# Second layers of four chunks as seven block products instead of eight, with x scaled before the transpose

## The chip, the cores and the metric

The kernel runs on one core of one Trainium2 chip. The metric is device time in microseconds for one execution of the whole kernel; lower is better. The engines are named as the profile names them: TensorE (PE) multiplies, VectorE (DVE), ScalarE (ACT) and GpSimd (POOL) do elementwise work, and SP issues transfers; GpSimd issues transfers on a queue of its own.

## The reference

```python
def _attn_ref(q, k, v, f_logit):                 # q, k, v, f_logit: (4, 8, 768, 48)
    f = 1.0 / (1.0 + np.exp(-f_logit))
    for t in range(S):
        state = f[:, :, t, :, None] * state + np.einsum('bhd,bhe->bhde', k[:, :, t], v[:, :, t])
        y[:, :, t] = np.einsum('bhd,bhde->bhe', q[:, :, t], state)

def _moe_ref(x, domain_probs, w1, w2):           # x: (3072, 384), w1: (4, 384, 1024), w2: (4, 1024, 384)
    p = domain_probs / (domain_probs.sum(-1, keepdims=True) + 1e-09)
    for e in range(E):
        h = np.maximum(x @ w1[e], 0.0)
        out += p[:, e:e + 1] * (h @ w2[e])

x = attn_out.transpose(0, 2, 1, 3).reshape(B * S, H * D)      # 3072 tokens of 384
```

A gated linear recurrence over 768 steps gives one row of 384 numbers for each token. Each row then goes through four experts of two layers, and the four results are added, weighted by probabilities.

## The kernel before, in words

The 768 steps are cut into six chunks of 128, numbered 0 to 5. A chunk holds 128 steps of each of the four batches, so 512 tokens. For every chunk there are two pieces of work.

*Attention* of a chunk, per batch `b`: the gates go through an exponential and a logarithm (`gate1`, `gate2` on ScalarE), are summed over the steps by a matmul (`pe_cs`, step `cs`), and exponentials of the sums (`exps`) scale q and k (`product`, mostly on GpSimd). Scaled q and k are transposed, in chunks 1 (second half) to 5 by a DMA transpose on SP (`dma_tp`, tile `QK`). Then come the scores (`pe_at`, step `at`), masked copies of them (`ev_at`, tile `AT`, on VectorE), the outputs (`pe_y`, step `y`), a bf16 copy of y (`yb`) and its DMA transpose into `xT` (`dma_xt`, three blocks of 128). `pe_kv`, `ev_kv` and `state` carry the recurrent state `Sf` and its bf16 copy `Sb` to the next chunk. v is loaded in float32 and cast (`cast_v`), except in chunk 0, where GpSimd's queue casts it in the transfer.

*Experts* of a chunk: the first layer `mm_h` makes 128 hidden rows for 512 tokens with three matmuls of 512 columns; `relu` copies them to `h` in bf16, on ScalarE or VectorE. There are 8 such units for each of 4 experts. The second layer `mm_o` makes 128 tokens x 384 outputs with eight matmuls of 384 columns. `ev_o` multiplies by the probability and adds to `o`; after the last expert the tile is stored. Chunk 1 is worked in halves of 256 tokens.

The attention of chunk c+1 is laid among the experts of chunk c. The order isn't written out by hand. A planner (`Plan`) gets every step with a cost for each engine that may do it, a priority, the steps that it depends on, and the buffers that it takes and frees (`rooms` says how many there are of each kind). `Plan.run` plays this through and hands out the steps: an engine that is free takes the step of lowest priority number that is ready. The instructions are then issued in that order on each engine, and each engine works its queue in order, so a step that is late holds up what stands behind it. `unit[0]` counts the units of expert work and serves as the scale of priorities; `base` sets where the attention of the next chunk begins on it. PSUM banks are in two pools of four: `ps_m` for the experts and `ps_t` for the attention.

The lines of the profile that matter below: L374 is the matmul of `mm_h`, L389 that of `mm_o`, L385 and L383 are `relu` on ScalarE and VectorE, L396, L398 and L400 are `ev_o`, L329 is `ev_at`, L336 and L340 are `pe_y`, L346 is `pe_kv`, L353 is `ev_kv`, L360 and L361 are `state`, L301 is `product`, L226 and L228 are copies (`yb` and others), L314 and L318 are the two DMA transposes, L237 and L233 are loads, L246 loads weights, L404 is the store.

## Time and profile before

| | before |
|---|---|
| median of 3 runs | 298.79 us (298.46 to 300.08) |
| span of the profiled execution | 296.6 us |
| TensorE matmuls busy in it | 289.0 us (97%), 2172 instructions |
| weight loads | 170.0 us (57%) |
| ScalarE | 174.3 us (59%), 317 instructions |
| VectorE | 126.1 us (43%), 250 instructions |
| GpSimd | 106.1 us (36%), 180 instructions |
| matmuls of the second layer (L389) | 776, 152.6 us |
| matmuls of the first layer (L374) | 708, 152.8 us |

The span is that of one profiled execution; the timed runs are of the same program, and their median lies 2.2 us above that span. Engines work at the same time, so busy times don't add up to the span. In the groups of the page, the time after the bar is the sum of the instructions, with the mean of one in ns, and then the idle time of that engine just before them. Matmuls follow each other in a pipeline, so the mean of one is longer than the distance from one to the next.

### The profile page before, as it was taken

The page shows a single profiled execution, that of the slowest core. Times are in us where ns is not written, and L with a number is a line of the kernel's source. Part 1 is how long each engine was busy: PE and PEld are TensorE (multiplying, and loading weights), DVE is VectorE, ACT ScalarE, POOL GpSimd, SP SyncE. Part 2 cuts the span into 40 slices and gives each one's busy share as a digit, 9 for nine tenths or more (in the row PEclk, how much of TensorE's full clock was granted, in tenths as well). Part 3 has the DMA queues.
Part 4 walks back from the last instruction along what each step waited for, and adds up shares of the span by engine and source line. Part 5 has one row for each costly group of instructions (what it writes and reads, how often), then busy time and mean ns, then how long its engine had stood idle before and what let it go on. Part 6 is the DMA issues. An engine that isn't in the chain of part 4 may idle for free.

```text
span 296.6 us, 5591 instructions
## 1 busy us (share of the span) xinstructions
PE 289.0 (97%) x2172; PEld 170.0 (57%) x2172; DVE 126.1 (43%) x250; ACT 174.3 (59%) x317; POOL 106.1 (36%) x180
## 2 busy tenths in 40 slices
PE   6899999999999999999999999999999999999995
PEld 2476555567777775555555555555555555555553
DVE  6786012785763673045375235243523222101223
ACT  5656656666684667777477575554475544465440
POOL 5786401138767448144449372243220000000000
PEclk9999999999999999999999999999999999999999
DMA  7999999998979999998979932102432100200002
GB/s 157 200 169 206 207 192 210 189 210 167 201 152 166 191 171 185 209 187 164 198 133 218 179 60 35 27 0 67 122 61 30 27 2 27 80 2 0 0 2 106
DMA packets 136462, 36.43 MB, mean 123 GB/s; under 512 B 126812, under 2 KB 135644, under 8 KB 136436
## 3 DMA queue, kind: packets, MB, share of 16 engines
q1 hardware_dynamic: 125188, 29.35, 52.0%
q0 software_dynamic: 11248, 6.72, 16.4%
q8 instruction: 17, 0.28, 0.4%
q14 instruction: 9, 0.07, 0.1%
HBM read 31.51 MB, written 4.72 MB: 122 GB/s over the span
## 4 chain that ended last, share of the span: by engine, by line
PE 78%; DMA 14%; POOL 3%; SPq 2%; issue 1%; ACT 1%; DVE 0%; POOLq 0%
PE ps_m L389 37%; PE ps_m L374 35%; DMA w_sb<-in_moe_w_dram 10%; DMA k<-in_k_dram 4%; SPq L237 2%; POOL w_sb L246 2%; PE ps_t L325 2%; PE ps_t L340 1%; PE ps_t L336 1%; PE ps_t L273 1%; POOL vb L233 1%; PE ps_t L346 1%; ACT e L293 1%; DVE o L396 0%; ACT xT L226 0%
## 5 line engine op out<-in xcount | busy, mean ns | idle before, releaser
L385 ACT ACTIVATE h<-ps_m 128x512 bf16<-128x512 f32 (+2 forms) x188 | 102.4, 548 | 91.9 <-PE ps_m L374 88.9
L374 PE MATMUL ps_m<-xT,w_sb 128*128 128x512 bf16 (+3 forms) x708 | 152.8, 339 | 0.6 <-ACT xT L226 0.6
L389 PE MATMUL ps_m<-w_sb,h 128*128 128x384 bf16 (+1 forms) x776 | 152.6, 324 | 0.1
L389 PEld LDWEIGHTS <-h 128*128 128x128 bf16 x776 | 75.0, 98 | 59.0 <-DMA w_sb<-in_moe_w_dram 0.3
L396 DVE SCALAR_TENSOR_TENSOR o<-ps_m,pn,o 128x384 f32<-128x384 f32 (+1 forms) x73 | 44.5, 612 | 117.3 <-PE ps_m L389 111.1
L374 PEld LDWEIGHTS <-w_sb 128*128 128x128 bf16 x708 | 65.3, 98 | 43.5 <-issue 0.7
L301 POOL TENSOR_TENSOR qk<-q,e 128x384 bf16<-128x384 f32 x18 | 21.4, 1195 | 36.5 <-ACT e L293 34.3
L360 POOL TENSOR_TENSOR Sf<-Sf,egs 48x192 f32<-48x192 f32 x40 | 20.2, 504 | 36.5 <-DVE Sf L353 34.4
L329 DVE TENSOR_TENSOR AT<-ps_t,mask 128x512 bf16<-128x512 f32 x48 | 30.2, 683 | 5.1 <-PE ps_t L325 5.1
L383 DVE TENSOR_SCALAR h<-ps_m 128x256 bf16<-128x256 f32 (+2 forms) x40 | 19.3, 499 | 26.5 <-PE ps_m L374 13.1
L293 ACT ACTIVATE e<-ps_t 128x384 f32<-128x384 f32 x48 | 26.7, 668 | 5.0 <-PE ps_t L273 3.5
L301 POOL TENSOR_TENSOR qk<-k,e 128x384 bf16<-128x384 f32 x20 | 20.2, 1013 | 8.7 <-ACT e L293 5.5
L353 DVE TENSOR_TENSOR Sf<-Sf,ps_t 48x192 f32<-48x192 f32 x40 | 14.0, 350 | 10.3 <-PE ps_t L346 9.4
L246 POOL DMA_DIRECT2D w_sb<-in_moe_w_dram x11 | 8.8, 807 | 18.5 <-DMA k<-in_k_dram 17.2
L361 POOL CAST sb<-Sf 48x192 bf16<-48x192 f32 x40 | 13.6, 340 | 2.6
L398 ACT ACTIVATE o<-ps_m,pn 128x384 f32<-128x384 f32 x22 | 12.8, 582 | 2.5 <-PE ps_m L389 1.5
L644 PE MATMUL ps_m<-busy 128*128 128x512 bf16 x34 | 10.9, 423 | 1.5 <-DVE busy L144 1.5
L265 ACT ACTIVATE ex<-f 128x768 f32<-128x768 f32 (+1 forms) x14 | 10.4, 746 | 1.8 <-DMA f<-in_f_logit_dram 1.8
L298 POOL DMA_DIRECT2D egs<-e x16 | 9.0, 563 | 6.9 <-ACT e L293 6.9
L340 PE MATMUL ps_t<-vb,AT 128*128 128x48 bf16 x192 | 11.4, 184 | 0.0
L269 ACT ACTIVATE gp<-ex 128x768 bf16<-128x768 f32 (+1 forms) x14 | 10.5, 751 | 0.3
L340 PEld LDWEIGHTS <-AT 128*128 128x128 bf16 x192 | 9.9, 97 | 1.1
(54 smaller groups left out, 120.6 us busy)
## 6 DMA issues: line engine op xcount, KB each, us to landing
out_dram<-o SPq DMA_DIRECT2D x23, 192.0 KB, 2.0
w_sb<-in_moe_w_dram POOLq DMA_DIRECT2D x5, 768.0 KB, 18.0
k<-in_k_dram SPq DMA_DIRECT2D x10, 384.0 KB, 5.6
q<-in_q_dram SPq DMA_DIRECT2D x10, 384.0 KB, 5.5
v<-in_v_dram SPq DMA_DIRECT2D x10, 384.0 KB, 5.7
f<-in_f_logit_dram SPq DMA_DIRECT2D x9, 384.0 KB, 4.6
w_sb<-in_moe_w_dram POOLq DMA_DIRECT2D x6, 384.0 KB, 9.0
f<-in_f_logit_dram SPq DMA_DIRECT2D x6, 192.0 KB, 3.8
```

The source lines that it names most:

```text
L246: ins["w", i] = nc.gpsimd.dma_start(out=w[:, e, ks, cols], in_=r[e][:, ks, cols])
L293: nc.scalar.activation(out=o, in_=i, func=AF.Exp, scale=1.0 if j else -1.0)
L301: engines[eng].tensor_tensor(out=tl("qk", c, b)[:, j, :, 0:D].rearrange("t (i r) d -> t i r d", r=2), in0=tl("qk"[j], c, b // 2)[:, hh(b), ...
L329: nc.vector.tensor_tensor(out=tl("AT", c, b)[:, r].rearrange("s i t -> s (i t)"), in0=tl("A", c, b, r).rearrange("s i t -> s (i t)"), in1= ...
L340: nc.tensor.matmul(out=y[:, h * D:(h + 1) * D], lhsT=AT[:, r, i, :], rhs=vb[:, h, :], start=(c == 0), stop=True, skip_group_check=True)
L353: nc.vector.tensor_tensor(out=Sf[rows, b], in0=Sf[rows, b], in1=KV[rows, :, r, :], op=ALU.add)
L360: nc.gpsimd.tensor_tensor(out=Sf[rows, b], in0=Sf[rows, b], in1=eg, op=ALU.mult)
L374: nc.tensor.matmul(out=hp(c, e, fc, n0, n1, nf)[:, f], lhsT=w1_sb[:, e, kk, (fc + f) * 128:(fc + f + 1) * 128], rhs=tl("xT", c)[:, kk, n0: ...
L383: nc.vector.tensor_relu(out=dst, in_=src)
L385: nc.scalar.activation(out=dst, in_=src, func=AF.Relu)
L389: nc.tensor.matmul(out=tl("op", c, e, nt, part)[:, cols], lhsT=tl("h", c, e, half_of(c, nt * T))[:, fc, nt * T:(nt + 1) * T], rhs=w2_sb[:, ...
L396: nc.vector.scalar_tensor_tensor(out=o, in0=op, scalar=pe, in1=o, op0=ALU.mult, op1=ALU.add)
```

## The change

For chunks 2 to 5 the second layer of a pair of experts is written as the product of two 2 x 2 block matrices: `h` in blocks of 256 tokens x 512 hidden rows, `w2` in blocks of 512 x 192. Seven block products with sums of blocks (`h_sum`, `w_sum`) take the place of eight. A product (`mm_p`) is 8 matmuls of 192 columns for each of two tiles of 128 tokens, and sums over the two experts of a pair in PSUM. `add_c` copies or adds the products into output tiles. So that products of two experts can be summed in PSUM, y is multiplied by each expert's probability before the transpose (`ev_x`): one copy of y for each expert, and two transposes of six blocks for each batch. In the middle of the kernel the products of one pair of experts stand between the first-layer units of the next pair (`group`).

In the same change the two pools of PSUM banks become one of seven, with the eighth from the first `mm_h` on; the buffers of f, q and k are halved, and others resized; v is loaded in every chunk by GpSimd's queue with the cast in the transfer, and its issue stands earlier; `Sb` is one tile instead of two; the mask is 128 x 128 and read four times over; `exps` of the gates are written in place; `busy` is 128 columns wide; and the attention of the next chunk begins earlier on the scale of units.

In the changed code the new lines are: L448 the matmul of `mm_p`, L436 `h_sum`, L425 `w_sum`, L455 the additions of `add_c` (plain copies are L223), L319 and L321 `ev_x`, L324 the transpose of six blocks, L458 the store, L230 v's load; `mm_h` is L387, `mm_o` L402.

The diff, cut to its core:

```diff
+        self.rooms["ps_t"] = self.rooms["ps_m"]
...
+                    if o.name == "h 0.0.0.0":
+                        self.rooms["ps_m"].append(7)
...
-    rooms = {"ps_m": 4, "ps_t": 4, "f": 4, "q": 4, "k": 4, "v": 4, "ex": 2, "gp": 4, "e": 3, "qk": 7,
-             "vb": 7, "egs": 8, "QK": 4, "AT": 2, "yb": 2, "xT": 2, "h": 2, "o": 6}
+    rooms = {"ps_m": 7, "ps_t": 0, "f": 2, "q": 2, "k": 2, "gp": 2, "e": 3, "qk": 6,
+             "vb": 4, "egs": 8, "QK": 3, "AT": 2, "yb": 3, "xT": 3, "h": 3, "s": 6, "o": 8}
+    S0 = 2
+    KH, DH, NG = KF // 2, Din // 2, E // 2
...
-    for i in range(2):
-        t = const.tile([MP, B, NP, 2 * D], BF16, name=f"sb{i}")
-        nc.vector.memset(t, 0.0)
-        Sb.append(t)
+    Sb = const.tile([MP, B, NP, 2 * D], BF16, name="sb")
+    nc.vector.memset(Sb, 0.0)
...
+    tw = wpool.tile([128, E, 3, KH, DH], BF16, name="tw")
...
-        if (c, nm) == (0, "v"):
-            ins[c, nm, b] = nc.gpsimd.dma_start(out=tl("vb", c, b), in_=srcs[nm][c, :, b * H:(b + n) * H, :])
-            if b < 2:
+        if nm == "v":
+            ins[c, nm, b] = nc.gpsimd.dma_start(out=tl("vb", c, b // 2).rearrange("t b h d -> t (b h) d")[:, hh(b, n), :],
+                                                in_=srcs[nm][c, :, b * H:(b + n) * H, :])
+            if c == 0 and b < 2:
...
-    def dma_xt(c, b):
-        nc.sync.dma_start_transpose(out=tl("xT", c)[:, :, b * T:(b + 1) * T], in_=tl("yb", c, b))
+    def ev_x(c, b, e, eng):
+        out, in_, pe = tl("yb", c, b, e // NG)[:, e % 2], tl("y", c, b)[:, 0:HD], pn[:, e, b * C + c:b * C + c + 1]
+        if eng == "ACT":
+            nc.scalar.activation(out=out, in_=in_, func=AF.Copy, scale=pe)
+        else:
+            nc.vector.tensor_single_scalar(out=out, in_=in_, scalar=pe, op=ALU.mult)
+
+    def dma_xt(c, b, g):
+        nc.sync.dma_start_transpose(out=tl("xT", c, g).rearrange("m e k t -> m (e k) t")[:, :, b * T:(b + 1) * T],
+                                    in_=tl("yb", c, b, g).rearrange("t e d -> t (e d)"))
+
+    def dma_x1(c, b):
+        nc.sync.dma_start_transpose(out=tl("xT", c)[:, 0, :, b * T:(b + 1) * T], in_=tl("yb", c, b)[:, 0])
...
+    def x_of(c, e):
+        return tl("xT", c, e // 2)[:, e % 2] if c >= S0 else tl("xT", c)[:, 0]
...
-                                 rhs=tl("xT", c)[:, kk, n0:n1], start=(kk == 0), stop=(kk == KD - 1))
+                                 rhs=x_of(c, e)[:, kk, n0:n1], start=(kk == 0), stop=(kk == KD - 1))
...
+    out_r = out.rearrange("(b c p) (u d) -> c u p b d", b=B, c=C, u=2)
+
+    def w_sum(e, j, eng):
+        b11, b12, b21, b22 = (w2_sb[:, e, i * KH:(i + 1) * KH, u * DH:(u + 1) * DH] for i in range(2) for u in range(2))
+        t2, t3, t4 = (tw[:, e, i] for i in range(3))
+        o, x, y = ((t3, b12, b22), (b12, b12, b11), (t2, b22, b12), (t4, b21, t2))[j]
+        engines[eng].tensor_tensor(out=o, in0=x, in1=y, op=ALU.subtract)
+
+    def blocks(c, e):
+        h = tl("h", c, e, 0)
+        return [h[:, i * KH:(i + 1) * KH, n * N2:(n + 1) * N2] for n in range(2) for i in range(2)]
+
+    def h_sum(c, e, j, eng):
+        a11, a12, a21, a22 = blocks(c, e)
+        s = lambda i: tl("s", c, e, i)
+        o, x, y, op = ((lambda: (s(1), a21, a22, ALU.add)), (lambda: (s(2), s(1), a11, ALU.subtract)),
+                       (lambda: (a21, a21, a11, ALU.subtract)), (lambda: (s(4), a12, s(2), ALU.subtract)))[j]()
+        engines[eng].tensor_tensor(out=o, in0=x, in1=y, op=op)
+
+    def bank(c, g, r):
+        return 5 if r == 3 and (c, g) == (C - 1, NG - 1) else r
+
+    def mm_p(c, g, r, u):
+        for n, e in enumerate(range(g * 2, g * 2 + 2)):
+            a11, a12, a21, a22 = blocks(c, e)
+            b11, b12, b21, b22 = (w2_sb[:, e, i * KH:(i + 1) * KH, v * DH:(v + 1) * DH] for i in range(2) for v in range(2))
+            a = {1: a11, 2: a12, 4: a22, 7: a21}[r] if r in (1, 2, 4, 7) else tl("s", c, e, {5: 1, 6: 2, 3: 4}[r])
+            w = {1: b11, 2: b21, 3: b22, 5: b12}[r] if r in (1, 2, 3, 5) else tw[:, e, {6: 0, 7: 1, 4: 2}[r]]
+            for fc in range(KH):
+                nc.tensor.matmul(out=tl("pp_", c, g, bank(c, g, r))[:, u], lhsT=a[:, fc, u * T:(u + 1) * T], rhs=w[:, fc],
+                                 start=(n + fc == 0 and bank(c, g, r) == r and (u == 0 or (c, g, r) != (C - 1, NG - 1, 5))), stop=(n == 1 and fc == KH - 1), skip_group_check=True)
+
+    def add_c(o, x, y, eng, us=slice(0, 2)):
+        if x is None:
+            copy(eng, o[:, us], y[:, us])
+        else:
+            engines[eng].tensor_tensor(out=o[:, us], in0=x[:, us], in1=y[:, us], op=ALU.add)
+
+    def store_c(c, i, j, o, us):
+        nc.sync.dma_start(out=out_r[c, j][:, 2 * i + us.start:2 * i + us.stop, :], in_=o[:, us])

...
+        for half in range(2 if c else 0):
+            p = slot(2 * half, 0) - 4
+            iv = P.add(f"v issue {c}.{half}", {"POOL": 1.25}, lambda _, half=half: load(c, "v", 2 * half, 2), p, takes=[("vb", c, half)],
+                       deps=[issued[-2 + half], kmul.get((c - 1, 2 * half + 1))], lag=7.0)
+            ld[c, "v", 2 * half] = ld[c, "v", 2 * half + 1] = iv
...
-                       deps=[G[b]], takes=[pt_("cs")], lag=0.2, frees=[("gp", c, half)])
+                       deps=[G[b], ydone.get((c - 1, b))], takes=[pt_("cs")], lag=0.2, frees=[("gp", c, half)])
...
-            vb = ld[0, "v", b] if c == 0 else P.add(f"v {c}.{b}", {"POOL": 0.5, "ACT": 0.52} if c == 1 else {"POOL": 0.5}, one(cast_v), s(4),
-                       deps=[ld[c, "v", b]], takes=[("vb", c, b)], frees=[("v", c, half)])
+            vb, kmul[c, b] = ld[c, "v", b], km
...
-                et = [P.add(f"tp {c}.{b}", {"DMA": 1.8}, on(dma_tp), s(4), deps=[qm, km], takes=[("QK", c, b)],
+                et = [P.add(f"tp {c}.{b}", {"DMA": 1.8}, on(dma_tp), s(4), deps=[qm, km, ydone.get((c - 1, B - 1))], takes=[("QK", c, b)],
...
             cs_ = lambda ks: slice(ks.start * 128, ks.stop * 128)
+            if c >= S0:
+                xdone[c, b] = {}
+                for g in range(NG):
+                    ex_ = [P.add(f"ev_x{e} {c}.{b}", {"ACT": 0.48, "DVE": 0.56}, lambda eng, b=b, e=e: ev_x(c, b, e, eng), s(11) + 0.1 + 0.01 * e,
+                                 deps=[y, pdone], takes=[("yb", c, b, g)], frees=[pt_("y")]) for e in (2 * g, 2 * g + 1)]
+                    xdone[c, b][g] = P.add(f"xt {c}.{b}.{g}", {"DMA": 1.5}, on(dma_xt, g), s(13), deps=ex_, takes=[("xT", c, g)],
+                                           frees=[("yb", c, b, g)], lag=3.0)
+                continue
...
-                  deps=[wd[e, 1][fc * len(wd[e, 1]) // KF]] + [t for b in xs for t in xdone[c, b]], takes=[key], lag=0.2, frees=[("xT", c)])
+                  deps=[wd[e, 1][fc * len(wd[e, 1]) // KF]] + ([xdone[c, b][e // 2] for b in xs] if c >= S0 else [t for b in xs for t in xdone[c, b]]),
+                  takes=[key, ("h", c, e, half_of(c, n0))], lag=0.2, frees=[("xT", c, e // 2) if c >= S0 else ("xT", c)])
...
+    ORDER = (1, 2, 4, 6, 7, 5, 3)
+    LAST = (1, 2, 5, 6, 7, 4, 3)
+    wsum, hsum = {}, {}
+
+    def add_wsum(e):
+        for j in range(4):
+            wsum[e] = P.add(f"w_sum{j} {e}", {"DVE": 0.62} if e < 2 else {"POOL": 2.1}, lambda eg, j=j: w_sum(e, j, eg), unit[0] + 6,
+                            deps=[omm[c, e, nt] for c in range(S0) for nt in range(B)] + [wsum.get(e)])
+
+    def add_sums(c, e):
+        fcs = lambda r: [hdone[c, e, fc, 0] for fc in r]
+        p = unit[0] + 0.3
+        s1 = P.add(f"s1 {c}.{e}", {"DVE": 0.75}, lambda eg: h_sum(c, e, 0, eg), p, deps=fcs(range(KF)), takes=[("s", c, e, 1)])
+        s2 = P.add(f"s2 {c}.{e}", {"DVE": 0.75}, lambda eg: h_sum(c, e, 1, eg), p + 0.01, deps=[s1], takes=[("s", c, e, 2)])
+        s3 = P.add(f"s3 {c}.{e}", {"DVE": 0.75}, lambda eg: h_sum(c, e, 2, eg), p + 0.02, deps=[s1])
+        s4 = P.add(f"s4 {c}.{e}", {"DVE": 0.75}, lambda eg: h_sum(c, e, 3, eg), p + 0.03, deps=[s2], takes=[("s", c, e, 4)])
+        hsum[c, e] = {1: fcs(range(KH)), 2: fcs(range(KH, KF)), 4: fcs(range(KH, KF)), 5: [s1], 6: [s2], 7: [s3], 3: [s4]}
...
+    def add_p(c, g, r):
+        es = (2 * g, 2 * g + 1)
+        key = ("ps_m", "pp_", c, g, bank(c, g, r))
+        end = (c, g) == (C - 1, NG - 1)
+        mm = []
+        for u in range(2):
+            frees = [("h", c, e, 0) if r in (1, 2, 4, 7) else ("s", c, e, {5: 1, 6: 2, 3: 4}[r]) for e in es]
+            mm.append(P.add(f"p{r} {c}.{g}.{u}", {"PE": 0.665}, lambda _, u=u: mm_p(c, g, r, u), unit[0] + 0.5 + 0.01 * u,
+                            deps=[s for e in es for s in hsum[c, e][r]] + [wsum[e] for e in es] + (mm or lastp + ([cdone[c]["r5"]] if end and r == 3 else [])), takes=[key], lag=0.2, frees=frees))
+        lastp[:] = mm[-1:]
+        src = lambda: tl("pp_", c, g, bank(c, g, r))
...
+        def read(nm, base, us=slice(0, 2)):
+            costs = {"ACT": 0.5, "DVE": 0.52} if base is None else {"DVE": 0.58 if us.stop - us.start == 2 else 0.4}
+            last[nm] = P.add(f"{nm} {c}.{g}.{r}", costs, lambda eg: add_c(o(nm), o(base) if base else None, src(), eg, us), p,
+                             deps=[mm[us.stop - 1], last.get(nm), last.get(base)], takes=[("o", c, nm)], frees=[key])
+
+        def plus(nm, other):
+            costs = {"DVE": 0.72, "POOL": 1.15}
+            if end:
+                costs.pop("POOL" if nm in ("u2", "u3", "c21") else "DVE")
+            last[nm] = P.add(f"{nm}+{other} {c}", costs, lambda eg: add_c(o(nm), o(nm), o(other), eg), p + 0.5,
+                             deps=[last[nm], last[other]], frees=[("o", c, other)])
+
+        def send(nm, i, j, us=slice(0, 2)):
+            P.add(f"store {c}.{nm}.{us.start}", {"DMA": 0.6}, lambda _: store_c(c, i, j, o(nm), us), p - 25, deps=[last[nm]], frees=[("o", c, nm)])
+
+        nm = {1: "u1", 2: "c11", 6: "u2", 7: "u3", 4: "c21", 5: "c22", 3: "c12"}[r]
+        if g == 0:
+            read(nm, "c22" if r == 3 else None)
+            return
+        if not (end and r == 3):
+            read(nm, nm)
+            last[f"r{r}"] = last[nm]
+        if r == 2:
+            plus("c11", "u1")
+            send("c11", 0, 0)
+        elif r == 6:
+            plus("u2", "u1")
+        elif r == 7:
+            plus("u3", "u2")
+            if not end:
+                plus("c21", "u3")
+                send("c21", 1, 0)
+            plus("c12", "u2")
+            if end:
+                plus("c22", "u3")
+                send("c22", 1, 1)
+        elif r == 4 and end:
+            plus("c21", "u3")
+            send("c21", 1, 0)
+        elif r == 5 and not end:
+            read("c12", "c12")
+            plus("c22", "u3")
+            send("c22", 1, 1)
+        elif r == 3 and not end:
+            send("c12", 0, 1)
+        elif r == 3:
+            for u in range(2):
+                us = slice(u, u + 1)
+                read("c12", "c12", us)
+                send("c12", 0, 1, us)
+
...
+    def group(c, g, prev, os=()):
+        os, ps = list(os), list(LAST if prev == (C - 1, NG - 1) else ORDER) if prev else []
+        for i in range(16):
+            if c is not None:
+                add_h(c, 2 * g + i // 8, i % 8, 0, NT, ALL)
+            if os:
+                add_o(*os.pop(0))
+            if ps and i in (0, 2, 3, 5, 6, 9, 12):
+                add_p(*prev, ps.pop(0))
+            if c is not None and i % 8 == 7:
+                add_sums(c, 2 * g + i // 8)
+            unit[0] += 1
...
-            base = u0 + {0: 10, 1: 0}.get(c, -6)
+            base = u0 + {0: 10, 1: 0, 2: -20}.get(c, -14)
...
-                for j, nm in enumerate("fkqv"):
+                for j, nm in enumerate("fkq"):
...
-            zip_units(hl(c + 1, 0, 0, NT, ALL), ol(c, E - 1, HI))
-        elif c == 2:
-            pass
+            for e in range(2):
+                add_wsum(e)
+            group(c + 1, 0, None, ol(c, E - 1, HI))
+            for e in range(2, E):
+                add_wsum(e)
         else:
-            zip_units(hl(c, 0, 0, NT, ALL), ol(c - 1, E - 1, ALL))
-        for e in range(E if c == 1 else 1, E):
-            zip_units(hl(c, e, 0, NT, ALL), ol(c, e - 1, ALL))
-    zip_units([], ol(C - 1, E - 1, ALL))
+            group(c, 1, (c, 0))
+            if c + 1 < C:
+                group(c + 1, 0, (c, 1))
+        if c < S0:
+            for e in range(E if c == 1 else 1, E):
+                zip_units(hl(c, e, 0, NT, ALL), ol(c, e - 1, ALL))
+    group(None, None, (C - 1, NG - 1))
```

## The prediction

> **What bounds the kernel now.** I read the page's busy rows and slices first, then what TensorE waited for, then the end of the chain of waits, then the busy time by stretches.
>
> ```profile
> span 296.6 us, 5591 instructions
> PE 289.0 (97%) x2172; PEld 170.0 (57%) x2172; DVE 126.1 (43%) x250; ACT 174.3 (59%) x317; POOL 106.1 (36%) x180
> ...
> PE   6899999999999999999999999999999999999995
> ...
> PEclk9999999999999999999999999999999999999999
> ```
>
> TensorE is full from the second slice to the last, at full clock. Since a busy PE isn't PE at its peak, I ask what it waited for, all its lines:
>
> ```profile
> PE ps_m L644 <- DVE busy L144: 1.5, 1, 1.5
> PE ps_t L273 <- ACT gp L269: 0.8, 2, 0.4
> PE ps_t L310 <- DVE qk L301: 0.6, 1, 0.6
> PE ps_m L374 <- ACT xT L226: 0.6, 1, 0.6
> PE ps_t L310 <- ACT QK L226: 0.2, 1, 0.2
> ```
>
> That is 3.7 us, all with the start of the program. The price of a matmul must come from the spacing, not from the rows' means (324 ns at L389), which include the pipeline. The chain in order of time gives it:
>
> ```profile
> 157.38 2.60 PE ps_m L389 x16
> 160.14 4.53 PE ps_m L374 x21
> ...
> 287.35 5.88 PE ps_m L389 x44
> 293.24 0.03 issue
> 293.26 0.42 DVE o L396
> ```
>
> L389 with 384 columns: 2.60/16 = 0.1625 us. L374 with 512: 4.53/21 = 0.2157 us. The last 44 are 28 of 384 columns (4.55 us) and 16 of 192, so one of 192 costs (5.88 - 4.55)/16 = 0.083 us. Each has a weight load of its own. The other engines, stretch by stretch:
>
> ```profile
> 140.00:160.00 20.00, 20.00 (x155) 11.54 (x154) 10.22 (x20) 11.87 (x19) 11.36 (x21) 1.00 0.90 175
> 180.00:200.00 20.00, 20.00 (x148) 11.07 (x147) 8.68 (x16) 9.74 (x18) 6.13 (x13) 1.00 0.05 11
> 220.00:240.00 20.00, 20.00 (x142) 10.91 (x141) 5.48 (x9) 10.87 (x19) 0.61 (x1) 1.00 0.19 30
> ```
>
> The columns are the stretch, then busy time of PE, PEld, DVE, ACT, POOL. VectorE and ScalarE are half free. TensorE's work is the time; what is taken from it comes off the end as long as the others can follow.
>
> **What the Trainium skill says.** (1) "VectorE: DVE Perf Modes", the perf-mode tier table: an elementwise operation of two bf16 tensors in SBUF takes two elements a cycle, one with an operand in PSUM one. Trace: L329 (512 from PSUM) 683 ns and L301 (384) 555 ns fit 1 ns an element and 0.18 us fixed. The two-a-cycle case is in no row. (2) "SBUF — State Buffer", Who interferes with whom: a VectorE instruction with two SBUF inputs contends with a GpSimd one that reads SBUF. One place of the trace agrees:
>
> ```profile
> 8.72 0.55 DVE L301 TENSOR_TENSOR qk<-q,e 128x384 bf16<-128x384 f32 x1
> 8.89 1.24 POOL L301 TENSOR_TENSOR qk<-k,e 128x384 bf16<-128x384 f32 x1 [0.19 <-ACT egs L295]
> ```
>
> The GpSimd product has a median of 1.00 us; here it overlaps a VectorE product and takes 1.24. VectorE, which began first, lost nothing. (3) "TensorE: Matmul & The Clock Gate", Back-to-back issue gap: pairs of weight load and matmul are said to be spaced 81 ns at 128 columns. The trace is faster: from 151.40 to 151.79 us twelve matmuls of `pe_y`, of 48 and 96 columns, started 33 ns apart, each with its load. So loads don't bound a matmul of 192 columns. (4) "PSUM — Partial Sum Buffer", The four PSUM rules: GpSimd can't read PSUM; no POOL row does. Every new read of a product falls on VectorE or ScalarE.
>
> **The change part by part.**
>
> *Second layers of chunks 2 to 5.* Removed: 4 chunks x 16 units x 8 matmuls, the last unit cut by columns, so 504 of 384 columns and 16 of 192: 504 x 0.1625 + 16 x 0.083 = 83.2 us. Added: 4 chunks x 2 pairs of experts x 7 products x 2 token tiles x 8 = 896 of 192 columns x 0.083 = 74.4 us. TensorE's other counts are unchanged. **-8.8 us**, all on the path.
>
> *VectorE's side, per chunk.* Removed: 16 `ev_o` x 0.61 and what it did of `ev_y`. Added, from the instruction order: 16 sums of 128x1024 bf16 (0.18 + 512 ns = 0.69 us; between this and 1.2 us at one element a cycle; I take 0.69 from the skill's table), 9 additions from PSUM (0.61 by L396), 3.5 SBUF additions (0.56 by L301), 7 of the scaled copies of y (0.61 by L400). With AT (8 x 0.68), Sf (8 x 0.35) and some 3 relus: 11.0 + 5.5 + 2.0 + 4.3 + 5.5 + 2.8 + 2.1 = 33 us. A chunk in the middle takes 45.0 us now (first `mm_h` of chunk 2 at 114.9, of chunk 3 at 160.0) and would take 45.0 - 2.2 = 42.8. So VectorE goes from about half to 78%, and ScalarE (28 relus x 0.60, 9 scaled copies x 0.58, exponentials 5.3, gates 3.4, 6 reads x 0.5) to 34 us, 79%. Both still fit beside TensorE, at nothing, with 9 us of room a chunk. If the cover went, each us of VectorE's excess would be one of TensorE.
>
> *Where the sums are waited for.* In the order the first product that needs a sum starts 4 us or more of TensorE work after the last `mm_h` of its experts; relu and two sums take 0.2 + 0.6 + 1.4. Nothing. In the last group p5 starts 2.7 us after the last `mm_h`, against 1.7 for relu, one sum and two hand-overs. Nothing.
>
> *Weight sums.* Experts 0 and 1: 8 on VectorE x 0.56 = 4.5 us once, after chunk 1. Experts 2 and 3: 8 on GpSimd, 768 elements, so about twice the product's 1.0: 16 us between the products of chunk 3. They're needed some 20 us later. Nothing, though GpSimd's products wait up to 2 us behind one.
>
> *x scaled before the transpose.* Four copies of y per tile instead of one, and two transposes of six blocks instead of one of three. SP needs 1.18 us to issue three blocks and 1.25 eight, landing in 2.3 and 3.6; six: 1.2 and 3.1 by interpolation. Queue: 16 more transposes, 19 us, against ten v loads gone from SP (10 x 1.3). Latency: in chunk 3 now the last y ends at 154.4, its copy at 154.96, the transpose lands 2.3 us later, and `mm_h` starts at 159.98: 2.7 us to spare. After the change the order puts 7.2 to 7.6 us of TensorE work between the last y of chunks 3, 4, 5 and the first `mm_h`; the way takes 0.2 + 0.6 (two copies, one on each engine; 1.2 in line) + 1.2 (a transpose of the tile before ahead on SP) + 3.1 = 5.1 to 5.7. About 2 us remain, in queues that are fuller, and TensorE runs in order: what is late stops it. I book **+0.9 us** (0.3 for each of three chunks; from 0 to 8).
>
> *One pool of PSUM banks.* TensorE work between a bank's last matmul and its next user: at least 1.94 us in chunks 2 to 5 now, 2.84 after, once 1.95. A gain in slack that has no wait to remove: nothing.
>
> *v a stage sooner, by GpSimd's queue with the cast in the transfer.* GpSimd loses 16 casts (0.51) and ScalarE 4, and issues ten loads (0.96 for half the size; about 1.3 each). The first is queued behind the weights, ahead of the last w2 piece, which also waits for k; at 59.2 us TensorE stood 0.3 us for that piece. Moved bytes are equal, so 0, between -0.3 and +1.
>
> *New order rules.* `cs` of a chunk is placed behind `y` of the one before on TensorE's own queue, which is no wait; the QK transposes of a chunk wait on SP for the last `y` of the one before. Behind them on SP stand loads, stores and that chunk's x transposes; the first `at` of chunks 3 to 5 comes 10 us or more of TensorE work after the wait ends. Nothing.
>
> *Half the buffers of f, q, k; fewer memsets; one state copy.* Loads start later but have a 43 us period for 6 us of transfer; `pe_kv` already waits for `pe_y`, so one Sb adds no wait. Nothing, in the start ±0.3.
>
> *The end.* Now the last store is issued 0.46 us after the last matmul. In the new order c22 (waiting for a GpSimd addition of about 1.1 us behind p7's two VectorE steps) and c21 stand before the last half of c12 on SP, at 0.33 each, and c21's addition before its read on VectorE: issued about 1.05 after. **+0.6 us.**
>
> Sum: 296.6 - 8.8 + 0.9 + 0.6 = 289.3 us of span; the median of the runs, 298.8, lies 2.2 above the profiled span: **291.5 us**.
>
> **The rivals.** *x comes late* (0.18): copies or transposes slip 2 to 3 us beyond the spare at the starts of chunks 3, 4, 5, so 3 x 2.2 on top: 298. For it: six blocks are unmeasured, and copies share engines that are 80% full. Against: transposes run unhindered after 180 us, where DMA is nearly idle.
>
> *VectorE becomes the bound* (0.16), the case that ends slower: the sums hold at one element a cycle or queue behind GpSimd's reads, 1.2 us instead of 0.69. That is 8.2 us more a chunk, 41 of 42.8 us. By the order the 20 us stretches of TensorE work in which y of chunks 4 and 5 is made hold 18 us of VectorE work already, with 8 to 12 sums; they'd need 22 to 24, and AT, which y waits for, stands in line. About 3.5 us over three chunks: 291.5 + 10.5 = 302. It turns the result when the added stops pass 7.3 us, at sums of about 1.05 us. For it: 48 of the 64 sums belong to chunks 2 to 4, in which GpSimd works. Against: in the one overlap seen GpSimd paid.
>
> *The products aren't cheaper* (0.04): at 98 ns each, the mean of a weight load's row, 896 take 87.8 us: 304. Decides at 92.9 ns (83.2/896). Against: the 83 and the 33 ns above.
>
> **How the numbers follow.** The forecast has 0.62, all of it faster by over 0.5%, which is about what a measurement of this kernel tells from no change. Half of late x is faster, half within; VectorE bound 0.14 slower, 0.02 within; dear products slower. Faster 0.71, same 0.11, slower 0.18. The range, 288.8 to 300.5, takes in no stall at all with a better start, and late x; it leaves out most of the slower cases. The likeliest case alone: 289.5 to 295.
>
> **What would show it.** Right: 896 matmuls of 192 columns spaced 83 ns; TensorE's waits still a few us; sums of 0.7 us; VectorE near 190 us busy (126 - 29 for `ev_o` - 6 for `ev_y` + 44 for the sums + 29 for additions + 17 for scaled copies + 4.5 for weight sums + 5 for relus). Wrong: sums above 1 us, `mm_h` waiting for xT transposes at the starts of chunks 3 to 5, `pe_y` waiting for AT, or a last store more than 2 us behind the last matmul.

## The result, and the profile after

The changed kernel takes **312.7 us** (median of 4 runs, 308.5 to 316.3) against 299.2 for the kernel before in the same session: a ratio of 1.037, with a 95% interval of 1.031 to 1.043. By that ratio it is slower by 11 us, where I had forecast 7 us faster. Two of its four runs, the profiled one among them, lie more than 1.5% above its shortest and are left out of the ratio, so differences between kernels are taken below from ratios (times 299 us) and not from medians. The profiled execution has a span of 314.5 us against 296.6. From its page, the same rows as before:

```profile
span 314.5 us, 6477 instructions
PE 286.9 (91%) x2522; PEld 196.6 (63%) x2548; DVE 198.6 (63%) x345; ACT 182.4 (58%) x343; POOL 139.5 (44%) x190
...
PE   7898999759999589998799899999999997999992
...
PEclk9999999998999979999799999999999999999998
```

TensorE's row is no longer a row of nines: it has holes in the 9th, 14th and 20th slice, and the clock has a dent, a stretch of some us at half speed, in or just behind each. The products themselves came out as planned. The chain of waits, in order of time, has

```profile
163.45 1.67 PE ps L387 x7
165.12 1.32 PE ps L448 x16
```

sixteen of 192 columns in 1.32 us, 0.083 each. What TensorE waited for, the first lines of a list of about 20 us (3.7 before; us in total, times, longest):

```profile
PE ps L375 <- ACT yb L223: 3.2, 1, 3.2
PE ps L402 <- DMA w_sb<-in_moe_w_dram: 2.7, 2, 1.7
PE ps L335 <- DMA QK<-qk: 1.7, 1, 1.7
PE ps L448 <- DVE h L396: 1.7, 1, 1.7
```

and the three stretches with the large stops (the stretch, busy time of PE, PEld, DVE, ACT, POOL, then the granted clock):

```profile
60.00:80.00 20.00, 15.07 (x130) 9.75 (x125) 9.40 (x20) 8.15 (x16) 9.80 (x15) 0.91 1.13 157
100.00:120.00 20.00, 15.05 (x156) 10.47 (x154) 12.39 (x26) 10.78 (x25) 5.98 (x14) 0.91 0.98 154
140.00:160.00 20.00, 16.64 (x157) 12.22 (x158) 17.26 (x22) 11.76 (x22) 14.45 (x17) 0.91 0.64 119
```

No engine is full in any of them: TensorE stands still while others wait for something too. The sum from 296.6 to 314.5, for this run: -8.8 for the products; +18.3 for stops between 20 and 300 us (19.0 us of TensorE's time not busy, 0.7 before); +5.4 for the clock, which falls to 0.91 of three stretches of 20 us (3 x 20 x 0.09); +2.2 for the end (last matmul to end of span 5.5 us, 3.3 before); -0.4 in the first 20 us. That makes +16.7 of 17.9; 1.2 us I can't place. This run is the longest of the four; the shortest has a span of 306.7 us at a mean clock of 0.992, against 0.981 here. The clock makes up some 3.5 of the 7.8 us between the two (314.5 x 0.019 less 306.7 x 0.008); the rest has no trace. The three stops are not peculiar to this run: `yb_five` below, whose four runs lie within 2.2 us of each other, has 15.5, 16.7 and 16.7 us busy in the same stretches.

**The stop at 62 to 70 us** has two parts. (`egs` is the 2 KB transfer that carries the last row of `e`, the exponentials, to where `state` reads it.)

```profile
54.51 1.15 POOL L230 DMA_DIRECT2D vb<-in_v_dram  x1
55.64 0.58 POOL L297 DMA_DIRECT2D egs<-e  x1
...
62.97 0.82 PE L402 MATMUL ps<-w_sb,h 128*128 128x384 bf16 x4 [1.73 <-DMA w_sb<-in_moe_w_dram]
...
67.70 1.16 ACT L292 ACTIVATE e<-ps 128x384 f32<-128x384 f32 x2 [5.41 <-DMA egs<-e]
...
69.28 0.34 PE L375 MATMUL ps<-ident,yb 128*128 128x128 bf16 x3 [3.20 <-ACT yb L223]
...
70.01 2.52 PE L402 MATMUL ps<-w_sb,h 128*128 128x384 bf16 x8
```

First TensorE waits 1.7 us for the last piece of w2. Then it waits 3.2 us for the copy of y, which stands on ScalarE behind two exponentials; these wait 5.4 us for a buffer of `e`, which is free only when the egs transfer that reads it has landed. That transfer was issued on GpSimd's queue at 55.64, right behind a load of v, and landed 12 us later; the slowest of the kernel before took 5.2. When TensorE goes on, eight matmuls of 384 columns take 2.52 us, 0.315 each instead of 0.1625: that is the dent in the clock.

**The stop at 104 to 111 us** begins with scaled copies of y. ScalarE's waits have this line:

```profile
ACT yb L319 <- DMA xT<-yb: 6.4, 3, 4.2
```

`yb` has three buffers and a tile of y needs two. The third is free when the transpose that reads it has landed, 2.9 us in the median after its issue, and SP issues the transposes one after another. Copies on ScalarE and VectorE stand behind the one that waits, relus among them. TensorE's own two large waits there are 1.7 us for a transpose of q and k and 1.6 for a VectorE instruction behind such a copy. This is the y of chunk 2.

**The stop at 146 to 152 us** is VectorE's and GpSimd's:

```profile
143.55 1.19 POOL L300 TENSOR_TENSOR qk<-q,e 128x384 bf16<-128x384 f32 x1
143.67 4.17 DVE L436 TENSOR_TENSOR s<-h 128x1024 bf16<-128x1024 bf16 x1
144.69 1.00 POOL L300 TENSOR_TENSOR qk<-k,e 128x384 bf16<-128x384 f32 x1
145.65 1.63 POOL L425 TENSOR_TENSOR tw<-w_sb 128x768 bf16<-128x768 bf16 x1
```

A sum of 0.69 us takes 4.17: it ends 0.56 us after the third of three GpSimd instructions, each of which had begun before the one ahead of it ended. Behind it on VectorE stand relus, copies and AT, for which TensorE waits 1.4, 0.9, 0.4 and 0.4 us.

### The profile page after: what moved, and what is told of

It reads as the page before. It is cut to its first block, busy times and chain, and to the rows that moved or that the text cites. A ratio compares the mean times of both kernels' runs of the same rounds, so it can differ in the third digit from the quotient of the medians.

```text
span 314.5 us, 6477 instructions
## 1 busy us (share of the span) xinstructions
PE 286.9 (91%) x2522; PEld 196.6 (63%) x2548; DVE 198.6 (63%) x345; ACT 182.4 (58%) x343; POOL 139.5 (44%) x190
## 3 DMA queue, kind: packets, MB, share of 16 engines
q0 software_dynamic: 31888, 8.69, 27.0%
## 4 chain that ended last, share of the span: by engine, by line
PE 40%; DVE 7%; DMA 2%; issue 1%; ACT 1%; DVEq 0%; ACTq 0%
PE ps L387 19%; PE ps L448 19%; DVE s L436 2%; DMA xT<-yb 2%; DVE h L396 1%; DVE AT L339 1%; DVE yb L321 1%; ACT yb L319 1%; PE ps L350 1%; PE ps L346 1%; PE ps L335 1%; DVE o L455 0%; PE ps L356 0%; DVE h L436 0%; PE ps L272 0%
## 5 line engine op out<-in xcount | busy, mean ns | idle before, releaser
L387 PE MATMUL ps<-xT,w_sb 128*128 128x512 bf16 (+3 forms) x682 | 141.1, 340 | 4.3 <-DVE o L225 1.4
L398 ACT ACTIVATE h<-ps 128x512 bf16<-128x512 f32 (+2 forms) x183 | 97.8, 545 | 58.4 <-PE ps L387 53.3
L387 PEld LDWEIGHTS <-w_sb 128*128 128x128 bf16 x708 | 66.3, 99 | 50.7 <-issue 3.4
L402 PE MATMUL ps<-w_sb,h 128*128 128x384 bf16 x256 | 52.7, 338 | 4.8 <-DMA w_sb<-in_moe_w_dram 2.7
L448 PEld LDWEIGHTS <-h 128*128 128x128 bf16 x512 | 43.2, 99 | 6.8 <-DVE h L396 1.9
L402 PEld LDWEIGHTS <-h 128*128 128x128 bf16 x256 | 25.2, 101 | 22.1 <-issue 5.0
L455 POOL TENSOR_TENSOR o<-o,o 128x384 f32<-128x384 f32 x10 | 10.2, 1026 | 62.7 <-DVE o L455 58.0
L448 PEld LDWEIGHTS <-s 128*128 128x128 bf16 x384 | 32.1, 98 | 6.0 <-issue 1.1
L292 ACT ACTIVATE e<-ps 128x384 f32<-128x384 f32 x48 | 26.6, 668 | 12.8 <-DMA egs<-e 8.7
L409 DVE SCALAR_TENSOR_TENSOR o<-ps,pn,o 128x384 f32<-128x384 f32 x24 | 14.8, 616 | 30.1 <-PE ps L402 29.9
L339 DVE TENSOR_TENSOR AT<-ps,mask 128x512 bf16<-128x512 f32 x48 | 30.3, 682 | 3.7 <-PE ps L335 3.6
L319 ACT ACTIVATE yb<-ps,pn 128x384 bf16<-128x384 f32 x36 | 19.9, 581 | 20.2 <-DVE yb L321 9.7
L321 DVE TENSOR_SCALAR yb<-ps,pn 128x384 bf16<-128x384 f32 x28 | 17.0, 616 | 22.1 <-ACT yb L319 15.1
L300 POOL TENSOR_TENSOR qk<-q,e 128x384 bf16<-128x384 f32 x18 | 23.0, 1282 | 15.7 <-ACT e L292 15.5
L436 DVE TENSOR_TENSOR s<-h 128x1024 bf16<-128x1024 bf16 x16 | 16.9, 1056 | 19.1 <-ACT h L398 18.8
L455 DVE TENSOR_TENSOR o<-o,ps 128x384 f32<-128x384 f32 (+1 forms) x36 | 18.6, 538 | 15.0 <-PE ps L448 10.4
L396 DVE TENSOR_SCALAR h<-ps 128x256 bf16<-128x256 f32 (+2 forms) x45 | 23.4, 536 | 7.3 <-PE ps L387 6.7
L448 PE MATMUL ps<-w_sb,h 128*128 128x192 bf16 x256 | 23.8, 246 | 1.7 <-DVE h L396 1.7
L448 PE MATMUL ps<-tw,h 128*128 128x192 bf16 x256 | 24.7, 250 | 0.0
L448 PE MATMUL ps<-w_sb,s 128*128 128x192 bf16 x256 | 24.1, 246 | 0.0
```

Source lines behind the costliest of these rows:

```text
L292: nc.scalar.activation(out=o, in_=i, func=AF.Exp, scale=1.0 if j else -1.0)
L300: engines[eng].tensor_tensor(out=tl("qk", c, b)[:, j, :, 0:D].rearrange("t (i r) d -> t i r d", r=2), in0=tl("qk"[j], c, b // 2)[:, hh(b), ...
L319: nc.scalar.activation(out=out, in_=in_, func=AF.Copy, scale=pe)
L339: nc.vector.tensor_tensor(out=tl("AT", c, b)[:, r], in0=tl("A", c, b, r), in1=mask01.unsqueeze(1).broadcast_to([T, NP, T]), op=ALU.mult)
L387: nc.tensor.matmul(out=hp(c, e, fc, n0, n1, nf)[:, f], lhsT=w1_sb[:, e, kk, (fc + f) * 128:(fc + f + 1) * 128], rhs=x_of(c, e)[:, kk, n0:n ...
L396: nc.vector.tensor_relu(out=dst, in_=src)
```

## The experiments

Ratios are to the kernel before, with 95% intervals; the changed kernel's own is 1.037 (1.031 to 1.043).

**1. The disputed costs by themselves.** `micro` has no diff; its parts are in the expectation.

> A kernel of its own, which computes none of the reference's outputs: 12 sums of 128x1024 bf16 on VectorE and 12 additions of a PSUM bank, 6 products (128x384) and 6 weight sums (128x768) on GpSimd, each alone and then beside each other, and after that blocks of 48 matmuls of 512 columns between which TensorE has to wait for 0 to 8 copies on ScalarE. Theory (each waits for the other at the SBUF they share, and VectorE for more than one instruction): a sum takes 0.69 us alone, over 1.2 us in the mean beside GpSimd's back-to-back work, with single ones of 2 to 4 us; the additions with one operand in PSUM keep their time. Rival 1 (GpSimd pays, as the prediction had it): sums stay at 0.7, products go from 1.0 to 1.3 or more. Rival 2 (the long sums of the changed kernel waited for a semaphore, not for SBUF): both keep their times. For the clock: after a stop of 3.5 us or more 16 matmuls run at 0.43 us instead of 0.216, that is 3.4 us at half clock; after a stop of less than 1.5 us none; between the two it is open.

VectorE's groups of twelve: sums alone, beside products, beside weight sums, and additions from PSUM beside products:

```profile
5.59 8.68 DVE L48 TENSOR_TENSOR s<-h 128x1024 bf16<-128x1024 bf16 x12
44.00 12.03 DVE L48 TENSOR_TENSOR s<-h 128x1024 bf16<-128x1024 bf16 x12
57.93 15.23 DVE L48 TENSOR_TENSOR s<-h 128x1024 bf16<-128x1024 bf16 x12
74.41 7.02 DVE L51 TENSOR_TENSOR o<-o,bank 128x384 f32<-128x384 f32 x12
```

The sums lose 3.4 us to six products and 6.6 us to six weight sums; the additions keep their 0.58. GpSimd pays too: six products took 8.06 us instead of 6.36 beside the sums, six weight sums 11.90 instead of 10.20. Both sides pay, so the rival on semaphores is out. The longest sum was 2.0 us: `micro` shows the contention, but not a sum held by several instructions in a row. That stands in the traces of whole kernels alone (4.17 us here, 4.18 in `yb_five`, 4.19 in `v_in_long_runs`). The blocks of 48 matmuls, each with the stop ahead of it in brackets:

```profile
144.72 10.52 PE L70 MATMUL acc<-x,xw 128*128 128x512 bf16 x47 [2.58 <-ACT x L72]
247.43 13.32 PE L70 MATMUL acc<-x,xw 128*128 128x512 bf16 x47 [3.20 <-ACT x L72]
264.56 13.28 PE L70 MATMUL acc<-x,xw 128*128 128x512 bf16 x47 [3.82 <-ACT x L72]
```

All five blocks behind stops of 3.2 to 5.1 us were 2.2 to 2.9 us longer, less than the 3.4 that I expected (16 x 0.216). Both behind 2.58 us kept 10.52; of the two behind 1.96 us one kept it and one lost 1.7. So a stop of 3.2 us cost 6 here; each of the three stretches with stops in the changed kernel cost 1.8 on top of them. The Trainium skill states the rule ("TensorE: Matmul & The Clock Gate", What's actually happening): half clock after an idle window of about 3.4 us, whose start doesn't depend on the program. `micro` agrees in the main, though one loss came behind 1.96 us, shorter than that window. In the changed kernel the second and third dent follow single stops of at most 1.7 us, with a few short matmuls between them; no run separates what counts there.

**2. One edit at a time on the changed kernel, and v's part alone on the kernel before.**

```
egs_by_sp        -  nc.gpsimd.dma_start(out=tl("egs", c, b)[:, 0:NP], ...
                 +  nc.sync.dma_start(out=tl("egs", c, b)[:, 0:NP], ...
wsum_by_vector   -  {"DVE": 0.62} if e < 2 else {"POOL": 2.1}, ... w_sum
                 +  {"DVE": 0.62}, ... w_sum
v_alone (in the kernel before: load, vb's shape, add_v and attention as in the change)
                 -  copy(eng, tl("vb", c, b), tl("v", c, b // 2)[:, hh(b), :])
                 +  ins[c, nm, b] = nc.gpsimd.dma_start(out=tl("vb", c, b // 2)...
```

> The changed kernel with the egs transfers issued on SP's queue at the same place of the order instead of GpSimd's, nothing else. Theory (egs is late because it stands behind v's load and the last weights on GpSimd's queue, so the e buffers come free late): egs lands in 2 to 5 us at most, the stops of TensorE at 62 and 66 to 69 us (5 us together) and the half clock after them (1.7 us) go, 5 to 7 us less than the changed kernel, so about 306. Rival (the stop comes from elsewhere, or egs is then held on SP behind transposes): TensorE is busy 15 to 16 us of the stretch 60 to 80 as before, 311 to 314.

308.6 us, 1.032 (1.026 to 1.038), 1.5 us less than the changed kernel and within the two intervals: TensorE is busy 18.7 of the 20 us from 60 to 80, but only 15.4 from 80 to 100. The stop moved on. Egs landed after 8.5 us at the longest, not after 5 as the theory had it.

> The changed kernel with the weight sums of experts 2 and 3 on VectorE too, and planned there at 0.62 us; the planner orders chunk 2's and 3's work anew from that. Theory (GpSimd's weight sums of 1.65 us hold VectorE's sums): no sum over 2 us between 130 and 165 us, TensorE's idle time in 140 to 160 falls from 3.4 to under 1 us, no half clock there, 3 to 5 us less than the changed kernel, so about 308. Rival (VectorE is simply full there, so that 8 x 0.55 = 4.4 us more on it make it worse, or GpSimd's products hold the sums as well): the stretch stays as it is or loses 1 to 3 us more, 312 to 316.

311.8 us, 1.043 (1.041 to 1.046): nothing won, 2 us lost. The stretch 140 to 160 went from 16.6 to 18.2 us busy and no sum took over 1.7 us, as the theory had it (so it is in every run below that has all weight sums on VectorE), but the two earlier stops stayed (16.2 and 15.7) and stops of 2 us came up at 200 and 240.

> The kernel before with one part of the change only: v by GpSimd's queue with the cast in the transfer, a stage sooner, in place of SP's load and the casts. Theory (this part by itself delays egs and the last weights on that queue): egs lands in up to 8 to 12 us instead of up to 5.2, TensorE stops for 3 to 5 us between 60 and 75 us, 302 to 306. Rival (the kernel before has 4 buffers' worth of slack there, the delay needs the other parts): egs is late but TensorE doesn't stop, 297.5 to 300.

**310.0 us, 1.038 (1.034 to 1.041).** This one part costs the kernel before as much as the whole change does. Its stretches 60 to 80 and 100 to 120 have 16.6 and 17.9 us busy, each with the clock at 0.91; TensorE waits 2.5 us for the last w2 piece, and egs lands after 11 us. The prediction had booked it at nothing. The issue of that piece, which waits on GpSimd for the landing of a load of k, in the kernel before and then here, with the load of v that is new ahead of it:

```profile
50.37 0.94 POOL L246 DMA_DIRECT2D w_sb<-in_moe_w_dram  x1 [17.25 <-DMA k<-in_k_dram]
...
24.09 1.14 POOL L233 DMA_DIRECT2D vb<-in_v_dram  x1 [1.05 <-DMA w_sb<-in_moe_w_dram]
52.30 0.94 POOL L247 DMA_DIRECT2D w_sb<-in_moe_w_dram  x1 [19.21 <-DMA k<-in_k_dram]
```

SP issued that load of k at 42.1 us in both; with v under way it let the piece go 1.9 us later.

**3. Why v's loads cost so much.** v1_by_sp is v12_by_sp with `VSP = (1,)`.

```
v12_by_sp          + VSP = (1, 2)
                   - if nm == "v":
                   + if nm == "v" and c not in VSP:
v_alone_egs_by_sp  v_alone and the edit of egs_by_sp
```

> A kernel of its own, which computes none of the reference's outputs: eight loads of v (two tiles each, runs of 192 bytes) in turn on SP's queue as float32, on GpSimd's as float32, on GpSimd's with the cast to bf16; then eight of q on SP's queue together with eight of v, once by GpSimd with the cast and once by SP; then one 2 KB egs transfer alone on GpSimd's queue, one behind two v loads on GpSimd's queue, one on SP's queue beside two v loads on GpSimd's. Theory A (the loads on GpSimd's queue cost the DMA engines more: from the queue rows of the kernel before and of the run with v alone, 31 ns a packet instead of 13): eight loads with the cast take about twice as long as by SP, and the pair q with v likewise; float32 on GpSimd's queue tells if queue or cast does it. Theory B (order on one queue): egs alone lands in 2 to 3 us, behind two loads in 5 us or more, on SP's queue beside them in 3. Rival: loads take the same time on either queue, and egs is not held up.

Eight loads took 16.9 us by SP, 17.4 by GpSimd and 15.1 by GpSimd with the cast, so theory A falls: neither queue nor cast makes a load alone dearer. egs landed in 1.9 us alone, 3.9 behind two loads on GpSimd's queue and 2.0 on SP's queue beside them: theory B's direction, but 2 us are little beside the 11 lost. What differs is a load of the other queue. q landed every 4.5 us while v ran beside it, against 1.8 ahead of v on one queue; sixteen loads took 35.4 us on two queues, 30.9 on SP's alone. VectorE's waits for the loads, by SP alone and then on two queues:

```profile
24.01 0.17 DVE L38 COPY one<-v 128x8 f32<-128x8 f32 x1 [1.62 <-DMA v<-in_v_dram]
...
88.82 0.17 DVE L38 COPY one<-q 128x8 f32<-128x8 f32 x1 [4.59 <-DMA q<-in_q_dram]
```

The Trainium skill says so ("DMA: Bandwidth & Descriptors", Queues, rings and completion order): each DMA engine takes its queues in turn, a packet of each. The direction agrees; an even share would have been 3.6 us (2 x 1.8), and the rest of the 4.5 is not explained. On SP's queue v stood behind k and q of its half; on a queue of its own it takes its turn at once.

> The kernel before with v by GpSimd's queue (as v_alone) and the egs transfers on SP's queue. Theory B (v's part costs what egs loses behind v on one queue): no stop over 1 us between 60 and 75 us, 299 to 302 instead of 310. Theory A (v's loads take more of the DMA engines' time wherever egs stands): the stops stay or move, 304 to 309.

310.9 us, 1.040 (1.035 to 1.045): theory B falls as well. With egs away from v the stop stays (14.8 us busy in 60 to 80), so the wait for `e` in the trace is not what v's 11 us hang on.

> The changed kernel with v of chunks 1 and 2 loaded as float32 on SP's queue, into the space in which the weight sums are formed later, and cast as in the kernel before; v of chunks 3 to 5 still by GpSimd's queue. Theory (v's loads on GpSimd's queue while DMA is full, before 120 us, make the first two stops): TensorE loses under 1.5 us between 55 and 100 us, egs lands within 5 us, but SP has four loads more ahead of chunk 2's transposes, so a stop of 2 to 6 us near 117 us takes its place: 303 to 308. Rival (the other parts make the stops): busy 15 to 16 of 20 us in 60 to 80, 311 or more.

311.3 us, 1.040 (1.035 to 1.046). Half a hit, the places by the theory and the time by the rival: from 20 to 100 us TensorE is now full (80.0 of 80), and the stops moved behind 100 us (16.1, 15.8 and 18.3 busy), where by the order SP has the loads of v ahead of chunk 2's transposes.

> As the run with v of chunks 1 and 2 on SP's queue, but chunk 1 alone. Theory: the stop of 3 us and more at 62 to 70 us goes (v of chunk 1 is what stood before egs there), the one at 104 to 111 us stays in part: 305 to 309. Rival: v of chunk 2, issued near 60 us, now holds egs instead, and nothing is won: 311 or more.

317.5 us, 1.064 (1.058 to 1.070), worse than the changed kernel, with the same picture: full up to 100 us, then 14.2 and 16.9. A miss; that the order after 100 us has no slack would fit, but the cause stays open.

**4. v later, and v in fewer packets.**

```
v_late, v_alone_late  - deps=[issued[-2 + half], kmul.get((c - 1, 2 * half + 1))], lag=7.0)
                      + deps=[issued[-1], kmul.get((c - 1, 2 * half + 1)), ld[c, "q", 2 * half]], lag=7.0)
v_in_long_runs, v_alone_long_runs
                      + in_=w1_r[c % E][:, b // 2, 0:2 * H * D]
v_late_wsum_vector    v_late and the edit of wsum_by_vector
```

> The kernel before with v by GpSimd's queue and the cast in the transfer, but each load ordered behind the q load of its own half of the chunk, about where SP's load of v stood, instead of a stage sooner. Theory C (a load of v issued a stage sooner takes its share of the DMA engines from k, q and f, which are needed first, as the pair in dma_alone showed: q landed every 4.5 us instead of 1.8 while v ran on the other queue): the stops go for the most part, 299 to 303 instead of 310. Rival D (two queues at once lose throughput whenever they meet, or a weight or egs is held by v wherever v stands): 306 to 311.

307.4 us, 1.029 (1.024 to 1.033), in rival D's range: the earlier place accounts for 2.6 of the 11 us, though the last w2 piece is issued at 49.9 again. Most of the cost stays with v on the second queue.

> The changed kernel with the same edit: v's loads of chunks 1 to 5 ordered behind the q load of their half. Theory C: the stop at 60 to 70 us and the one at 104 to 111 go for the most part, what is left is VectorE held by GpSimd at 140 to 160 and the first matmuls after it: 300 to 306. Rival D: 309 to 314.

308.4 us, 1.028 (1.021 to 1.035), between the theory and the rival, 2.6 us less than the changed kernel: 60 to 80 is full again (19.8), later stretches lose about 2 us each.

> The changed kernel with v's loads of chunks 1 to 5 at their places and of their size, but read in one run of 3 KB a partition (rows of the first layer's weights stand in for v, so y is not the reference's) instead of 16 runs of 192 bytes: 10 loads of 2048 packets become 10 of a sixteenth. Theory (what the loads cost is DMA engines' time for small packets): a load lands in half the time or less, the stops before 120 us shrink by half or more: 302 to 307. Rival (order on GpSimd's queue alone, or SP's transposes, make the stops): 310 to 314.

304.4 us, 1.018 (1.014 to 1.023): the packets of GpSimd's queue fall from 31888 to 12688, and 5.5 us go.

> The kernel before with v by GpSimd's queue (as v_alone), but v's loads of chunks 1 to 5 read in one run of 3 KB a partition instead of 16 of 192 bytes (rows of the first layer's weights stand in for v, so y is not the reference's). Theory (it is the small packets on a second queue): nearly all of the 11 us goes, 297 to 301. Rival (order on GpSimd's queue: egs and the last weights behind a bulk load): half or more stays, 304 to 309.

303.7 us, 1.018 (1.014 to 1.023): between theory and rival. The many packets are about 6 of v's 11 us. In what is left ScalarE's gates wait up to 3.3 us for f. That f is late because v was issued sooner would fit, but is only argued: late and long loads together were not run.

> The changed kernel with v's loads ordered late (as v_late) and all weight sums on VectorE (as wsum_by_vector). Theory: the gains of the two add, since one lies before 120 us and the other after: 2 to 5 us less than v_late, 297 to 302. Rival (VectorE is full after 120 us, as in the run with the weight sums alone): the same as v_late or more.

307.5 us, 1.027 (1.020 to 1.034): the rival. TensorE is nearly full up to 100 us and then loses 5.2 us in 140 to 160 and 1 to 2 us in six other stretches; the waits name copies into `yb` behind xT transposes (one of 2.3 us at 206 us).

**5. Buffers, and everything together.**

```
yb_five     - "yb": 3, ... "o": 8
            + "yb": 5, ... "o": 7
            - praw = const.tile([NR, T, E], FP32)
            + praw = wk.tile([NR, T, E], FP32, name="s0")
four_fixes  v_late_wsum_vector, praw as above, and
            + "e": 4, "qk": 5, ... "yb": 4, ... "o": 7
            - {0: 10, 1: 0, 2: -20}.get(c, -14)
            + {0: 10, 1: 0, 2: -20}.get(c, -20)
```

> The changed kernel with five buffers of yb instead of three (room for them from o, seven instead of eight, and from the raw probabilities, which are put where a buffer of s lies later). Theory (a scaled copy of y waits until the transpose that reads its buffer has landed, which the planner doesn't count): no copy into yb waits for a transpose, the stops at 104 to 111 us and those of 1 to 2 us at the later chunks' starts shrink: 4 to 7 us less, 305 to 308. Rival (SP issues the transposes no faster, so x comes as late as now, or VectorE is the cause): 310 to 314.

308.1 us, 1.031 (1.029 to 1.034). The mechanism came as the theory had it: no copy into `yb` waits for a transpose any more. The gain did not: 1.6 us by the ratios, within the intervals, where 4 to 7 were expected. The stop at 62 to 70 stays, as it should; 100 to 120 goes from 15.1 to 16.7 busy, and the 1.7 us at 262 are gone.

> The changed kernel with v's loads ordered behind the q load of their half, all weight sums on VectorE, four buffers each of yb and e instead of three (from o 7, qk 5 and the raw probabilities' place), and the attention of chunks 4 and 5 placed six units earlier. Theory (the causes are separate and add): 298 to 303, since v's packets still cost on the second queue. To beat the kernel before it would have to come under 297, for which I see no more than one chance in five.

**297.3 us, 0.995 (0.993 to 0.997): 1.5 us under the kernel before**, and 12.5 us under the changed kernel.

```profile
span 294.8 us, 6467 instructions
PE 281.3 (95%) x2519; PEld 194.2 (66%) x2548; DVE 193.5 (66%) x344; ACT 185.6 (63%) x352; POOL 128.1 (43%) x182
...
PE   7999999999999979989999999999999999999992
```

TensorE's row is closed again but for 3.3 us between 100 and 140 us; between 20 and 280 us it isn't busy for 5.7 us in all, 0.7 before. These stops and an end that is 2.2 us longer take most of the 8.8 us that the products save. VectorE has 66% of the span and isn't the bound. The same fixes with v back on SP's queue in every chunk, as in the kernel before, were not run.

**6. One cause put back.** Each run undoes one edit of four_fixes.

> four_fixes with v's loads put back a stage sooner, as in the changed kernel. Theory (v's loads ahead of k, q and f on a full DMA make the first stops, whatever the buffers): 5 to 10 us more, 302 to 307. Rival (the fourth buffers take the delay up): 297 to 300.

304.6 us, 1.020 (1.015 to 1.025): **+7.5 us**, nearly all of it before 120 us (17.0, 17.6 and 17.4 busy).

> four_fixes with the weight sums of experts 2 and 3 back on GpSimd. Theory (GpSimd's 1.65 us operations hold VectorE's sums, and TensorE stops at 140 to 160 us): 2 to 6 us more, 299 to 303. Rival (with the buffers there is slack enough to take a late sum): 297 to 298.5.

1.020 (1.012 to 1.028), **+7.5 us**, from only two runs, 302.9 and 306.8 us. Its profile is of a run of 308.0 us. It shows 3.0 us lost in 140 to 160, behind sums of up to 2.9 us, and 1.8 at half clock after it; another stop of 3.7 us at 80 to 100 lies before any weight sum and can't be due to them. So about 5 us have a place in the trace, the rest hasn't.

> four_fixes with three buffers of e instead of four. Theory (an e is held until the egs transfer that reads it has landed, 4 us in the median and more early on): 1 to 5 us more, 298 to 302. Rival (with v late egs lands soon enough for three): 297 to 298, and then the fourth yb and the earlier attention are what v_late_wsum_vector lacked.

298.2 us, 0.996 (0.994 to 0.999): the rival; the fourth `e` can't be told from nothing. What v_late_wsum_vector (1.027) lacked is then the fourth `yb` together with the earlier attention: **9 us** (1.027 to 0.996). The two were not separated, nor from the buffers of `qk` and `o` that make room for `yb`.

The three add up to 24 us, about twice the 12.5 that they take off together, and taken away one at a time from the changed kernel they gave from -2 to +2.6. So they do not add. TensorE works in order, and what one stop delays hides the next: the stops that moved on (egs_by_sp, v12_by_sp) fit this, but it is my reading.

## Why the prediction was wrong

- *Second layers, -8.8 us*: right, 0.083 us a matmul. The rival "not cheaper" is out. In four_fixes, at nearly full clock, TensorE is busy 7.7 us less than before.
- *v a stage sooner, "0, between -0.3 and +1"*: **the step that failed first**, in the words "Moved bytes are equal, so 0". I counted its bytes and its instructions on GpSimd's queue, and named the last w2 piece behind it. (The 0.3 us that I gave TensorE there is a weight load's wait of 0.32; between the matmuls lie 0.15.) I didn't ask whom the transfer displaces on DMA engines that were full to 120 us. Alone it measured +11 us on the kernel before, and its early place +7.5 in four_fixes. Of the 11, long runs take off 5.7 and the later place 2.6, each alone; the rest is open. That egs holds `e` I hadn't seen either, but moving egs or adding a buffer of `e` won nothing that could be told from none.
- *VectorE's side, "at nothing, with 9 us of room a chunk", and weight sums, "nothing, though GpSimd's products wait up to 2 us"*: the totals were good (198.6 us against about 190; median sum 0.69), the reading wrong. The mean room says nothing of a sum that waits for three GpSimd instructions in a row. I had the direction half wrong too: I quoted the Trainium skill ("SBUF — State Buffer", Who interferes with whom) and then believed the one overlap in which GpSimd paid. The same section says that the order of issue decides who blocks. That agrees with the trace, where GpSimd's instruction began 0.12 us ahead of the sum, but the sum waited for two more. My rival had the mechanism, but as a mean of 1.2 us over all sums; the mean of the slowest group was 1.06, and bursts did the harm.
- *x scaled before the transpose, +0.9 (0 to 8)*: mis-sized. I worked out the time from y to x, for chunks 3 to 5 alone, but not when `yb` is free again, and the largest stop came with chunk 2. The planner takes the buffer as free 1.7 us after the issue of the transpose begins (1.5 and 0.2); it is free when that lands, 2.9 us after the issue in the median and 6.8 at the longest. Together with the attention's place it is 9 us in four_fixes.
- *The end, +0.6*: +2.2. The order was as I said, c21's addition and store ahead of c12's, but the last store was issued 2.3 us behind the last matmul, not 1.05.
- *Missing altogether*: the clock, 5.4 us in the profiled run, and 2.5 and 4.3 by the mean clock (0.992 and 0.986) of the two runs in the ratio. I wrote that "each us of VectorE's excess would be one of TensorE".
- *One pool of banks, order rules, half buffers*: not tried alone.

The range ended too low because each doubt was priced as if the others' slack stayed. The resources of two rivals, the copies of y and VectorE's sums, made trouble together, with a third that wasn't among the rivals; but neither came as written. No `mm_h` waits for a transpose in the list of TensorE's waits, and VectorE, busy 63% of the span, is not the bound.

## What to carry to other kernels

A transfer that moves to another queue is not free because its bytes are equal: list what is on the DMA engines at that time and is needed sooner, and which buffers wait for a landing on either queue. When the engine that sets the time loses its cover, price each stop with what follows it: here three stretches with 3 to 5 us of stops cost 1.8 us more each. Test causes by putting them back into a version in which all are gone: taken away one at a time they showed 2.6 us or less, put back 7 to 9.
